# Attention and two gated MLPs on one core: V's global rows loaded into place, V's copies shared with VectorE, and a planner with other prices for the DMA queue

## The chip, the core and the metric

The kernel runs on one core of one Trainium2 chip. The metric is the device time of one execution in microseconds; less is better. TensorE (PE) does the matmuls, VectorE (DVE), ScalarE (ACT) and GpSimd (POOL) the elementwise work, and SyncE (SP) issues every DMA of this kernel, one after the other from one queue.

## The reference, cut to what matters

```python
# batch 4, heads 8, 512 local and 32 global rows per head, head dim 64
out_g = softmax(q_g @ k_all.T / 8) @ v_all          # global rows see everything
s_ll  = where(|i - j| <= 32, q_l @ k_l.T / 8, -1e9) # local rows: a band ...
s_l   = concat([q_l @ k_g.T / 8, s_ll])             # ... and the global keys
out_l = softmax(s_l) @ concat([v_g, v_l])
x = concat([out_g, out_l]) as (2176, 512)           # 4 x 544 tokens
x = x / rms(x) * rms_g
y = (silu(x @ w_gate) * (x @ w_val)) @ w_out        # 512 -> 1536 -> 512
z = (sigmoid(y @ w2_gate) * (y @ w2_val)) @ w2_out  # 512 -> 1536 -> 512
```

The weights arrive as 64-bit floats and are taken apart as two 32-bit words each.

## The kernel before

The local rows are 16 tiles T of 128 rows, four to a batch. Each tile's steps are tasks with names. `lk`, `lq` and `lv` load K, Q and V; `k`, `q` transpose them on TensorE, `kc`, `qc` copy them out of PSUM. `a1` makes the scores of four blocks of 32 rows, each against its band and the 32 global keys, beginning with eight matmuls that write the mask. `mx`, `ex` are row minimum (the scores carry a minus sign) and exponential, `a2` the transpose of the probabilities, `pc` its copy, `a3` the product with V, `nm` the division by the sum. Then follow the RMS norm (`sq`, `ms`, `sc`), the split in two fp16 halves in a staging tile `xs` (`xh` the upper half, `xm` the lower), and `xl`, a transposing DMA from `xs` into the resident operands `xhi`. The global rows of each batch take a path of their own (`sg`, `g1`, `g1x`, `g2`, `g3`, `gx`); `g3` reads V's global rows from a tile `vg`.

For `a3`, V must lie in an order of its own. `vw` is two buffers, even tiles in one and odd tiles in the other; each holds four blocks of keys for the four blocks of rows. A tile of V lies in `vt` (six buffers). Task `("vw", T, n)` copies piece n into `vw`: n = 0 and 1 are 64x1040 elements, n = 2 to 5 are 32x520. Pieces 6 to 9, the global rows, are needed for the first two tiles of a batch alone, since the buffers keep them. Each piece waits until `a3` of tile T-2 has read the buffer. In the kernel before, the four quarters of `vg` are loaded by `load_vg` with four DMAs a batch, and pieces 6 to 9 are copied from there; for T > 1 the planner chooses GpSimd or a DMA for each piece, for T = 0 and 1 GpSimd or VectorE.

The order on all engines is made by a planner in the kernel while it is built. Class `Booked` books each instruction on a clock `now` of its engine with a price; for SP it also books when the data land (`land`). `choose` takes, of the tasks whose inputs are there, the one that can start first within a margin, by priority. Where TensorE would wait longer than `fill`, it puts idle matmuls (`b<-ident` 128x256) in front. Priorities and some prices stand in a table `PR`. `gemm` is a stream of matmuls of the first MLP (`xhi` by `wgv`, then `hhi` and `hlo` by `wo`) that the planner weaves into the attention once `xl` of three tiles has been done. After the attention (`attend`) the rest is written in order, and between matmuls `give` hands out jobs for the other engines: taking weights apart (`c_ops`, `s_ops`) and combinations for a fast product (`jobs`). Nearly every instruction has the line of the recording helper, L145 here and L149 after.

```python
def vw_eng(T, n):
    return "ps" if T > 1 else "pd"
...
        xs_t[T] = ap.tile([128, 2, DM], F16, tag="xs", name="xs", bufs=1)
...
        task(("xh", T), "ad", lambda e: st_xh(T, e), P("xh"), ("sc", T), ref("xl", T - 1), c=(520, 341))
```

Of the kernel before, what the change touches and what calls it, by code (L numbers as in the profile page):

```python
# [10 lines left out]
F32 = mybir.dt.float32  # L11
F16 = mybir.dt.float16
# [9 lines left out]
def tile_attention_moe_moe(  # L22
# [64 lines left out]

    class Booked:
# [4 lines left out]
        def __getattr__(self, name):  # L93
            f = getattr(self.eng, name)

            def g(*args, **kw):
# [3 lines left out]
                ins = [x for x in aps if x is not out]  # L100
                n = max(int(np.prod(x.shape[1:])) for x in aps) if "axis" in kw else int(np.prod(out.shape[1:]))
# [11 lines left out]
                elif key == "s":  # L113
# [9 lines left out]
                    now["s"] = t + (1250 if kw.get("transpose") else 620 if ns[0] < 100000 else 560 + 0.11 * min(max(now["dma"] - t, 0), 6000))  # L123
# [54 lines left out]
    nc = Engines(tc.nc)  # L178
# [955 lines left out]
    def st_g3(b, e):  # L1134
        pt = pt_t.pop(("g", b, e))
        vg = vg_t[b]
        p = bank(("gn", b, e))
        for r in range(5):
            for pr in range(NPR):
                h = 2 * pr + e  # L1140
                if r < 4:
                    l, v = pt[:, r, 32 * pr:32 * pr + 32], vt_t[4 * b + r][:, h * DV:h * DV + D]
                else:
                    l, v = pt[0:SG, r, 32 * pr:32 * pr + 32], vg[0:SG, h * DV:h * DV + D]
                nc.tensor.matmul(p[32 * pr:32 * pr + 32, 0:D], l, v, start=(r == 0), stop=(r == 4))
        p_t["g", b, e] = p
# [45 lines left out]
    def warm(n):  # L1192
        p = bank()
        for i in range(n):
# [3 lines left out]
    PR = dict(lkg=-7.25, kgt=7.41, lqg=-1.98, qgt=3.21, gB=1.07, lk=-4.25, lq=-1.55, lv=-0.02, lg=-0.66,  # L1198
              q=3.87, qc=-16.93, k=0.24, k0=-8.51, nk=-2.48, kc=3.82, kc0=-0.72, a1=8.55, vw=0.09, e=2.04,
              mx=-5.17, ex=2.53, a2=-3.33, pc=-0.11, a3=-0.84, nm=-4.07, sq=15.55, ms=-7.09, sc=-0.86,  # L1200
              a4=-18.55, xh=5.81, xl=-8.54, sg=8.94, g=5.82, lv0=-0.76, lk1=-6.39, G=1000, post=-7.94,
              raw=-3.21, w0=0.24, w1=0.35, w2=12.08, w3=16.91, w4=17.64, w5=-6.83, w6=7.76, w7=26.25,
              w8=11.55, Le=146, Ld=62, La=106, Lp=5314538, Ls=1690, backlog=4477, fill=1035, guard=1, kcd=0,
              land=1190, vs0=24309, vs1=341, vs2=1815, xt=0.37)
# [17 lines left out]
    def ref(name, *a):  # L1222
        return (name, *a) if a[0] >= 0 else None
# [8 lines left out]
    def tile_tasks(T):  # L1232
# [6 lines left out]
        if t == 0:  # L1239
            task(("lg", b), "s", lambda e: load_vg(b), P(PR["lg"]),  # L1240
                 *([("vw", T - 8 + i, n) for i in range(2) for n in range(6, 10)] + [("g3", b - 2, 1)] if b >= 2 else []), after=ref("lg", b - 1))
# [10 lines left out]
        for n in range(len(vw_refs(T))):  # L1252
            v = vw_pieces(T)[n][1]
            task(("vw", T, n), vw_eng(T, n), lambda e, n=n: st_vw(T, n, e), P(PR["vw"]),
                 ref("a3", T - 2, 0), ref("a3", T - 2, 1), ("lg", b) if v is None else ("lv", v),
                 c=(1150 if n < 2 else 606, (616 if n < 2 else 345) if T < 2 else PR["vs0" if n < 2 else "vs1" if n < 6 else "vs2"]))
# [17 lines left out]
        task(("xh", T), "ad", lambda e: st_xh(T, e), P("xh"), ("sc", T), ref("xl", T - 1), c=(520, 341))  # L1274
# [20 lines left out]

    def build_tasks():
        for n, a, dst in (("kg", k_g, kgT), ("qg", q_g, qgT)):
# [12 lines left out]
        task(("xh", NT), "ad", lambda e: st_xh(NT, e), NT, ("sc", NT), ref("xl", NT - 1), c=(520, 341))  # L1310
# [231 lines left out]

    def run_op(key, op):
        e, f = (op.eng, op.f) if isinstance(op, Op) else (op[0] and op[0].lower(), op[1])
        f()
        if e:
            ready[key] = now[e] + 130

    def give():
        while True:  # L1550
            w_give()
            c = []
            for a in (0, 2, 1):
                if part_jobs[a]:
                    c.append((0.0, f"h{a}", part_jobs[a], 0))
            for key, ops in (("c", c_ops), ("s", s_ops)):
                if ops:
                    c.append((due_w(ops), key, ops, 0))
            for k in range(2):
                i = [i for i, x in enumerate(jobs) if x[0][1] == k]  # L1560
                if i:
                    key = jobs[i[0]][0]
                    if k == 0 or not any(x[0] == (key[0], 0) for x in jobs):
                        c.append((due_j(key), key, jobs, i[0]))
            for _, key, js, i in sorted(c, key=lambda x: x[0]):
                op = js[i][1][0] if js is jobs else js[0]
                if fits(key, op):
                    if js is jobs:
                        js[i][1].pop(0)
                        if not js[i][1]:  # L1570
                            js.pop(i)
                    else:
                        js.pop(0)
                    run_op(key, op)
                    break
            else:
                return
# [4 lines left out]
    with tc.manual_schedule():  # L1582
# [17 lines left out]
        w_go[0] = True  # L1600
        for wi, (g, ch, Ts) in list(enumerate(work))[at[0]:]:
# [68 lines left out]
```

## Time and profile before

| | |
|---|---|
| median of 3 runs | 894.03 us |
| lowest, highest | 889.8, 896.12 us |
| the profiled execution, its own time | 896.37 us |
| its span from first to last instruction | 894.5 us |
| mean granted TensorE clock | 0.994 |

The span is the profiled execution seen from inside; its own time holds 1.87 us more, ahead of and behind it. The three timed runs and the profiled one are single executions of the same program. A granted clock of 1 is 2.4 GHz, and the lower level is 1.2 GHz.

### The profile page before, as it was taken

How to read it: one execution, taken by the hardware profiler on the slowest of the kernel's cores; microseconds unless marked ns; L12 is line 12 of the kernel's file. 1: busy time of each engine (PE TensorE's matmuls, PEld its weight loads, DVE VectorE, ACT ScalarE, POOL GpSimd, SP SyncE). 2: the span in 40 equal slices, each digit the busy share in tenths (PEclk: the TensorE clock that was granted, in tenths of full speed). 3: DMA queues.
4: the chain of work that ended last, by engine and by line, in shares of the span. 5: the costliest groups of instructions: out<-in, count | busy, mean ns of one | idle time of the engine just before them, and what ended most of it. 6: DMA issues, size and time to landing. Idle time of an engine off the chain costs nothing.

```text
span 894.5 us, 18832 instructions
## 1 busy us (share of the span) xinstructions
PE 866.8 (97%) x7733; PEld 543.3 (61%) x7733; DVE 610.6 (68%) x1050; ACT 452.2 (51%) x986; POOL 266.7 (30%) x300
## 2 busy tenths in 40 slices
PE   8889798899999999999999999999999999999998
PEld 6667565666666666666666666556556565556553
DVE  4867767697788888788737877748764468645252
ACT  4886586565334445555527444546545264344230
POOL 2754445342211211121214446442202122212010
PEclk9999999999999999999999999999999999999999
DMA  9977879461000114131300121110331003000102
GB/s 211 170 153 145 172 151 185 117 139 63 1 25 23 50 46 124 54 107 48 95 1 1 56 88 48 48 48 28 114 106 37 1 24 95 1 1 13 59 33 98
DMA packets 108998, 66.56 MB, mean 74 GB/s; under 512 B 76912, under 2 KB 101488, under 8 KB 108912
## 3 DMA queue, kind: packets, MB, share of 16 engines
q1 hardware_dynamic: 108912, 65.36, 29.2%
q8 instruction: 61, 1.00, 0.5%
q14 instruction: 25, 0.20, 0.1%
HBM read 52.17 MB, written 4.46 MB: 63 GB/s over the span
## 4 chain that ended last, share of the span: by engine, by line
PE 80%; DMA 9%; DVE 4%; ACT 2%; SPq 1%; issue 1%; POOL 1%; DVEq 0%; ACTq 0%; POOLq 0%
PE p L145 66%; PE b L145 14%; DMA vt<-in_v_l_dram 3%; DMA xhi<-xs 2%; DMA q<-in_q_l_dram 1%; DMA vw<-vt 1%; SPq L145 1%; DVE wf L145 1%; DVE xs L145 1%; DMA k<-in_k_l_dram 1%; ACT s L145 1%; DMA vg<-in_v_g_dram 1%; DVE ya L145 0%; ACT pt L145 0%; DVE wc L145 0%
## 5 line engine op out<-in xcount | busy, mean ns | idle before, releaser
L145 PEld LDWEIGHTS <-wc 128*128 128x128 f16 x2556 | 250.1, 98 | 144.8 <-issue 1.4
L145 PE MATMUL p<-tt,wc 128*128 128x384 f16 (+1 forms) x1296 | 208.6, 317 | 0.6 <-ACT gv L145 0.4
L145 PE MATMUL p<-xhi,wc 128*128 128x384 f16 (+1 forms) x1260 | 205.2, 317 | 0.0
L145 POOL TENSOR_TENSOR h<-gv,h 128x384 f16<-128x384 f32 (+1 forms) x66 | 84.4, 1279 | 286.1 <-ACT h L145 274.1
L145 PE MATMUL p<-wo,h 128*128 128x512 f16 x612 | 133.4, 379 | 0.0
L145 ACT ACTIVATE gv<-p 128x384 f32<-128x384 f32 (+1 forms) x174 | 80.4, 469 | 76.0 <-PE p L145 69.6
L145 DVE SCALAR_TENSOR_TENSOR wf<-raw,wf 128x512 int32<-128x512 int32 x144 | 113.2, 794 | 2.2
L145 PEld LDWEIGHTS <-wo 128*128 128x128 f16 x864 | 84.3, 98 | 47.7 <-issue 0.2
L145 PEld LDWEIGHTS <-h 128*128 128x128 f16 x612 | 59.9, 98 | 71.1
L145 DVE SCALAR_TENSOR_TENSOR ya<-p,ya 128x384 f32<-128x384 f32 (+2 forms) x106 | 61.0, 581 | 54.7 <-PE p L145 53.9
L145 PE MATMUL b<-xhi,wgv 128*128 128x384 f16 (+1 forms) x576 | 93.3, 320 | 2.0 <-DMA xhi<-xs 2.0
L145 ACT ACTIVATE h<-gv 128x384 f16<-128x384 f32 (+3 forms) x93 | 54.7, 592 | 73.5 <-DVE gv L145 71.2
L145 DVE SCALAR_TENSOR_TENSOR gv<-gv 128x384 f32<-128x384 f32 (+3 forms) x81 | 66.7, 823 | 36.2 <-ACT gv L145 35.3
L145 PE MATMUL p<-h,wo 128*128 128x384 f16 (+1 forms) x576 | 90.0, 317 | 0.0
L145 DVE TENSOR_TENSOR gv<-p,gv 128x384 f32<-128x384 f32 (+1 forms) x108 | 55.4, 530 | 46.8 <-ACT gv L145 46.6
L145 PEld LDWEIGHTS <-wgv 128*128 128x128 f16 x576 | 56.2, 99 | 34.6 <-issue 1.8
L145 ACT ACTIVATE sa<-p 128x384 f32<-128x384 f32 (+1 forms) x54 | 24.7, 466 | 79.2 <-PE p L145 79.0
L145 ACT ACTIVATE wf<-raw 128x512 f32<-128x512 f32 x72 | 47.2, 671 | 27.9 <-DVE wc L145 13.5
L145 POOL COPY vw<-vt 64x1040 f32<-64x1040 f32 (+1 forms) x37 | 39.5, 1069 | 50.2 <-DMA vt<-in_v_l_dram 38.7
L145 POOL TENSOR_TENSOR sm<-wf 128x256 f32<-128x256 f32 x18 | 15.4, 858 | 119.9 <-DVE wc L145 87.3
L145 POOL TENSOR_TENSOR hlo<-t,hhi 128x384 f16<-128x384 f32 (+1 forms) x24 | 26.6, 1109 | 69.3 <-ACT hhi L145 69.1
L145 PE MATMUL b<-hhi,wo 128*128 128x384 f16 (+1 forms) x192 | 46.9, 317 | 0.0
(117 smaller groups left out, 1007.1 us busy)
## 6 DMA issues: line engine op xcount, KB each, us to landing
raw<-in_moe_w_gate_dram SPq DMA_DIRECT2D x24, 512.0 KB, 4.1
raw<-in_moe_w_val_dram SPq DMA_DIRECT2D x24, 512.0 KB, 3.7
raw<-in_moe_w_out_dram SPq DMA_DIRECT2D x24, 512.0 KB, 3.7
k<-in_k_l_dram SPq DMA_DIRECT2D x16, 256.0 KB, 3.9
q<-in_q_l_dram SPq DMA_DIRECT2D x16, 256.0 KB, 4.9
vt<-in_v_l_dram SPq DMA_DIRECT2D x16, 256.0 KB, 5.3
out_dram<-ya SPq DMA_DIRECT2D x16, 256.0 KB, 2.0
vw<-vt SPq DMA_DIRECT2D x54, 65.0 KB, 2.8
```

The source lines that it names most:

```text
L145: return f(*args, **kw)
```

## The change

Pieces 6 to 9 of `vw` are no longer copied from `vg`: each is a DMA from V's global rows in HBM straight into the buffer, always on SP. The column of ones beside V is written once into both buffers by a new task `ones`. `vg` is loaded once a batch instead of four times. The other pieces of tiles above 1 may now go to VectorE too (`"psd"`). `xs` gets a second buffer, and `xh` waits for `xl` of tile T-2 rather than T-1. The planner prices a DMA issue at 700 ns (620 before) or 620 ns and a share of the backlog (560), a transposing one at 1600 ns (1250), and a landing at 2243 ns after the data (1190). All numbers of `PR` are others, so the whole order of the attention moves. Behind the attention, `fill_in` is called before each instruction of VectorE or ScalarE that would wait, and puts a job into that wait if it fits. Of the new functions, `handout` and `take` are `give`'s old code cut out.

```diff
@@ class Booked
+                if key in "da" and between[0]:
+                    between[0](key, max([wrote.get(tag_of(x), 0.0) for x in ins] + [free0.get(out.tensor.name, 0.0)]))
...
-                    now["s"] = t + (1250 if kw.get("transpose") else 620 if ns[0] < 100000 else 560 + 0.11 * min(max(now["dma"] - t, 0), 6000))
+                    now["s"] = t + (1600 if kw.get("transpose") else 700 if ns[0] < 100000 else 620 + 0.11 * min(max(now["dma"] - t, 0), 6000))
@@ load_vg
-        vg_t[b] = ap.tile([128, H * DV], F32, tag="vg", name="vg", bufs=2)
-        nc.gpsimd.memset(vg_t[b].rearrange("p (h d) -> p h d", h=H)[:, :, D:DV], 1.0)
-        for i in range(4):
-            nc.sync.dma_start(out=vg_t[b][32 * i:32 * i + SG].rearrange("p (h d) -> p h d", h=H)[:, :, 0:D],
-                              in_=v_g[b].rearrange("h p d -> p h d"))
+        vg_t[b] = ap.tile([128, H, D], F32, tag="vg", name="vg", bufs=1)
+        nc.sync.dma_start(out=vg_t[b][0:SG], in_=v_g[b].rearrange("h p d -> p h d"))
@@ vw_eng, st_vw
-        return "ps" if T > 1 else "pd"
+        return "s" if n >= 6 else "psd" if T > 1 else "pd"
...
-        i = (vg_t[T // TPB] if v is None else vt_t[v])[r]
+        if v is None:
+            nc.sync.dma_start(out=o.rearrange("p (h d) -> p h d", h=H)[:, :, 0:D], in_=v_g[T // TPB].rearrange("h p d -> p h d"))
+            return
+        i = vt_t[v][r]
@@ st_xh
-        xs_t[T] = ap.tile([128, 2, DM], F16, tag="xs", name="xs", bufs=1)
+        xs_t[T] = ap.tile([128, 2, DM], F16, tag="xs", name="xs", bufs=2)
@@ PR (one line of nine)
-              w8=11.55, Le=146, Ld=62, La=106, Lp=5314538, Ls=1690, backlog=4477, fill=1035, guard=1, kcd=0,
+              Lp=570650794, Ls=1558, backlog=5956, fill=2110, guard=1, kcd=0, land=2243, vs0=28709, vs1=0,
@@ tile_tasks
-        task(("xh", T), "ad", lambda e: st_xh(T, e), P("xh"), ("sc", T), ref("xl", T - 1), c=(520, 341))
+        task(("xh", T), "ad", lambda e: st_xh(T, e), P("xh"), ("sc", T), ref("xl", T - 2), c=(520, 341))
@@ new
+    def st_ones():
+        for w in vw:
+            nc.gpsimd.memset(w.rearrange("p i (h d) -> p (i h) d", d=DV)[:, :, D:DV], 1.0)
+    def fill_in(e, t):
+        while t > now[e] + 200:
+            for _, key, js, i in handout():
+                ...
+                s = max([now[e], 0 if free else ready.get(key, 0)] + [wrote.get(tag_of(x), 0.0) for x in (ins() if ins else ())])
+                if s + took.get(f.__code__, 900) <= t + 250:
+                    take(key, js, i)
+                    break
+            else:
+                return
@@ behind the attention
         w_go[0] = True
+        between[0] = fill_in
```

Counted over the whole program, the instructions that change in number are these. TensorE: 59 fewer idle matmuls (29 instead of 88). VectorE: copies of 64x1040 into `vw` 16 instead of 2, of 32x520 3 instead of 6, and copies of `ptg` 8 instead of 5. GpSimd: 16 instead of 30 and 18 instead of 26. SP: loads of `vg` 4 instead of 16, loads of V's global rows into `vw` 32 instead of 0, copies of `vt` into `vw` 43 instead of 54, of `vg` into `vw` 0 instead of 10; 245 DMAs instead of 246.

SyncE's queue at the program's start, before (`x` holds the global K or Q rows, `raw` a half of a weight block, numbers tell buffers apart):

```order
L145 DMA k_144<-in_k_l_dram 128x8x64
L145 DMA k_146<-in_k_l_dram 128x8x64
L145 DMA raw_148<-in_moe_w_gate_dram 128x4x256
L145 DMA raw_155<-in_moe_w_gate_dram 128x4x256
L145 DMA raw_158<-in_moe_w_val_dram 128x4x256
L145 DMA k_185<-in_k_l_dram 128x8x64
L145 DMA x_191<-in_q_g_dram 32x8x64 x4
L145 DMA raw_200<-in_moe_w_val_dram 128x4x256
L145 DMA q_209<-in_q_l_dram 128x8x64
```

The same place after:

```order
L149 DMA k_146<-in_k_l_dram 128x8x64
L149 DMA k_148<-in_k_l_dram 128x8x64
L149 DMA x_150<-in_q_g_dram 32x8x64 x4
L149 DMA vt_163<-in_v_l_dram 128x8x64
L149 DMA q_172<-in_q_l_dram 128x8x64
L149 DMA k_180<-in_k_l_dram 128x8x64
L149 DMA raw_187<-in_moe_w_gate_dram 128x4x256
L149 DMA raw_198<-in_moe_w_gate_dram 128x4x256
L149 DMA raw_201<-in_moe_w_val_dram 128x4x256
L149 DMA vg_206<-in_v_g_dram 32x8x64
L149 DMA q_226<-in_q_l_dram 128x8x64
```

The load of the global Q rows, of V's first tile and of Q's first tile have moved ahead of the weights.

SyncE's queue around the first three transposing DMAs, before (here the second and the third stand, those of tiles 1 and 2):

```order
L145 DMA k_980<-in_k_l_dram 128x8x64
L145 DMA vt_995<-in_v_l_dram 128x8x64
L145 DMA q_1021<-in_q_l_dram 128x8x64
L145 DMA k_1034<-in_k_l_dram 128x8x64
L145 DMA vt_1083<-in_v_l_dram 128x8x64
L145 DMA_TRANSPOSE xhi0_73<-xs_1053 128x8x128
L145 DMA vw0_85<-vt_995 32x520 x3
L145 DMA vw0_85<-vg_729 32x520
L145 DMA vw0_85<-vt_1083 32x520
L145 DMA vw1_86<-vt_995 32x520
L145 DMA vw1_86<-vt_1083 32x520 x2
L145 DMA_TRANSPOSE xhi0_73<-xs_1258 128x8x128
```

After (all three stand here):

```order
L149 DMA vt_827<-in_v_l_dram 128x8x64
L149 DMA q_851<-in_q_l_dram 128x8x64
L149 DMA_TRANSPOSE xhi0_73<-xs_840 128x8x128
L149 DMA_TRANSPOSE xhi0_73<-xs_842 128x8x128
L149 DMA vg_965<-in_v_g_dram 32x8x64
L149 DMA vw0_85<-vt_655 32x520 x2
L149 DMA vw0_85<-vt_827 32x520
L149 DMA vw0_85<-in_v_g_dram 32x8x64 x2
L149 DMA_TRANSPOSE xhi0_73<-xs_1087 128x8x128
L149 DMA vw0_85<-in_v_g_dram 32x8x64 x2
```

The first two transposes now stand side by side, behind the loads of tile 6's Q, and the third follows six DMAs later; some of V's global rows are loaded ahead of it.

VectorE where the first `xs` tiles are made, before (`gmx`, `ptg` belong to the global rows):

```order
L145 COPY pt_1025<-b_975 128x512
L145 COPY ptg_1005<-b_987 32x128
L145 SCALAR_TENSOR_TENSOR x_747<-x_747,ms_993,gB_80 128x512
L145 CAST xs_1053<-x_747 128x512
L145 TENSOR_REDUCE gmx_1055<-b_1007 128x1
L145 TENSOR_REDUCE gmx_1055<-b_1008 128x1
L145 TENSOR_TENSOR gmx_1055<-gmx_1055 128x1
```

After:

```order
L149 SCALAR_TENSOR_TENSOR x_532<-x_532,ms_609,gB_80 128x512
L149 SCALAR_TENSOR_TENSOR x_701<-x_701,ms_771,gB_80 128x512
L149 CAST xs_840<-x_532 128x512
L149 CAST xs_842<-x_701 128x512
L149 TENSOR_TENSOR xs_840<-x_532,xs_840 128x512
L149 TENSOR_TENSOR xs_842<-x_701,xs_842 128x512
```

Two `xs` tiles are now made one inside the other, where before one stands alone.

## Rows read from the trace of the kernel before

**Rows 1.** The profile's page, part 1: busy time of each engine, share, instructions.

```profile
PE 866.8 (97%) x7733; PEld 543.3 (61%) x7733; DVE 610.6 (68%) x1050; ACT 452.2 (51%) x986; POOL 266.7 (30%) x300
```

**Rows 2.** Busy time in six stretches: length, engines, granted clock, DMA share, GB/s.

```profile
0.00:20.00 20.00, 17.73 (x131) 13.52 (x131) 8.97 (x15) 9.17 (x20) 4.28 (x26) 1.00 0.97 217
20.00:50.00 30.00, 26.71 (x808) 20.90 (x812) 25.98 (x59) 25.13 (x87) 20.50 (x33) 1.00 0.90 173
50.00:100.00 50.00, 43.91 (x1052) 32.42 (x1050) 33.32 (x78) 34.59 (x106) 27.05 (x42) 0.97 0.76 152
100.00:165.00 65.00, 54.97 (x1136) 38.57 (x1135) 44.90 (x94) 42.57 (x118) 33.75 (x46) 0.95 0.85 172
...
200.00:880.00 680.00, 679.44 (x4208) 411.43 (x4206) 464.89 (x751) 318.53 (x610) 168.07 (x139) 1.00 0.16 49
```

**Rows 3.** What TensorE waited for, 0 to 200 us: total us, times, longest.

```profile
PE b L145 <- DMA q<-in_q_l_dram: 6.3, 5, 2.6
PE b L145 <- DMA vw<-vt: 4.4, 5, 3.0
PE b L145 <- DMA xhi<-xs: 2.0, 2, 1.1
PE b L145 <- DVE wo L145: 1.8, 1, 1.8
PE b L145 <- DMA k<-in_k_l_dram: 1.8, 2, 1.5
```

**Rows 4.** TensorE in order of time: start, duration, instructions, wait ahead.

```profile
7.68 6.28 PE L145 MATMUL b<-ident 128*128 128x256 bf16 x56
...
19.65 0.30 PE L145 MATMUL b<-mask,ident 64*32 64x256 bf16 x8
...
31.62 1.41 PE L145 MATMUL b<-vw,pt 128*32 128x65 f32 x58
...
175.93 0.62 PE L145 MATMUL b<-vw,pt 128*32 128x65 f32 x20
```

**Rows 5.** SyncE's queue in order of time: start, duration, DMAs issued.

```profile
0.72 1.89 SPq L145 DMA_DIRECT2D x<-in_k_g_dram  x4
2.65 1.08 SPq L145 DMA_DIRECT2D k<-in_k_l_dram  x2
3.77 1.45 SPq L145 DMA_DIRECT2D raw<-in_moe_w_gate_dram  x2
...
7.85 3.69 SPq L145 DMA_DIRECT2D x<-in_q_g_dram  x4
```

**Rows 6.** Stretches of 5 us in which the granted clock was low.

```profile
55.00:60.00 5.00, 5.00 (x145) 4.32 (x147) 2.80 (x7) 3.74 (x13) 3.07 (x5) 0.74 0.51 117
...
140.00:145.00 5.00, 5.00 (x88) 3.05 (x87) 0.37 (x4) 2.10 (x7) 3.54 (x6) 0.70 1.00 155
...
160.00:165.00 5.00, 5.00 (x105) 3.86 (x94) 3.67 (x8) 1.40 (x3) 3.64 (x3) 0.66 0.91 217
```

**Rows 7.** Instructions that write vw: count, ns minimum/median/maximum, first and last.

```profile
L145 SPq DMA_DIRECT2D vw<-vt x54: 507/541/2257, 33.4 to 163.0; - x54
L145 POOL COPY vw<-vt x37: 606/1047/1981, 21.5 to 162.3; 64x1040 f32<-64x1040 f32 x30, 32x520 f32<-32x520 f32 x7
...
L145 DVE COPY vw<-vt x5: 684/751/1549, 21.7 to 31.4; 32x520 f32<-32x520 f32 x3, 64x1040 f32<-64x1040 f32 x2
```

**Rows 8.** VectorE's waits for the transposing DMA, 0 to 200 us.

```profile
DVE xs L145 <- DMA xhi<-xs: 8.2, 4, 4.6
```

**Rows 9.** SyncE's waits for TensorE, 0 to 200 us.

```profile
SPq L145 <- PE b L145: 25.8, 23, 2.8
```

**Rows 10.** The view of DMA issues: count, KB each, median us to landing.

```profile
q<-in_q_l_dram SPq DMA_DIRECT2D x16, 256.0 KB, 4.9
...
vw<-vt SPq DMA_DIRECT2D x54, 65.0 KB, 2.8
...
vg<-in_v_g_dram SPq DMA_DIRECT2D x16, 64.0 KB, 3.4
```

More of the change, by code (lines that the diff above doesn't have):

```diff
@@ L86, in fetched @@
         return came[min(i, len(came) - 1)] if i >= 0 else 0.0
+    between = [None]
     class Booked:
@@ L1143, in st_g3 @@
                 else:
-                    l, v = pt[0:SG, r, 32 * pr:32 * pr + 32], vg[0:SG, h * DV:h * DV + D]
+                    l, v = pt[0:SG, r, 32 * pr:32 * pr + 32], vg[0:SG, h]
                 nc.tensor.matmul(p[32 * pr:32 * pr + 32, 0:D], l, v, start=(r == 0), stop=(r == 4))
@@ L1240, in tile_tasks @@
             task(("lg", b), "s", lambda e: load_vg(b), P(PR["lg"]),
-                 *([("vw", T - 8 + i, n) for i in range(2) for n in range(6, 10)] + [("g3", b - 2, 1)] if b >= 2 else []), after=ref("lg", b - 1))
+                 *([("g3", b - 1, 0), ("g3", b - 1, 1)] if b else []), after=ref("lg", b - 1))
         task(("q", T), "e", lambda e: tr4(("q", T), q_t.pop(T).rearrange("p h d -> p (h d)"), ("qc", T)), P(PR["q"]), ("lq", T), ref("a1", T - 2) if PR["guard"] else None, banks=1)
@@ L1253, in tile_tasks @@
             v = vw_pieces(T)[n][1]
-            task(("vw", T, n), vw_eng(T, n), lambda e, n=n: st_vw(T, n, e), P(PR["vw"]),
-                 ref("a3", T - 2, 0), ref("a3", T - 2, 1), ("lg", b) if v is None else ("lv", v),
-                 c=(1150 if n < 2 else 606, (616 if n < 2 else 345) if T < 2 else PR["vs0" if n < 2 else "vs1" if n < 6 else "vs2"]))
+            vd = PR["vd"]
+            task(("vw", T, n), vw_eng(T, n), lambda e, n=n: st_vw(T, n, e), P(PR["vw" if n < 6 else "vz"]),
+                 ref("a3", T - 2, 0), ref("a3", T - 2, 1), ("ones",) if v is None else ("lv", v),
+                 c=(0,) if n >= 6 else (1150 if n < 2 else 606, 616 + vd if n < 2 else 345 + vd) if T < 2 else
+                 (1150 if n < 2 else 606, PR["vs0" if n < 2 else "vs1"], 616 + vd if n < 2 else 345 + vd))
         for e in range(2):
@@ L1294, in batch_tasks @@
         task(("gxc", b), "ad", lambda e: st_gxc(b, e), P(8), ("gx", b), c=(525, 607))
+    def st_ones():
+        for w in vw:
+            nc.gpsimd.memset(w.rearrange("p i (h d) -> p (i h) d", d=DV)[:, :, D:DV], 1.0)
     def build_tasks():
+        task(("ones",), "p", lambda e: st_ones(), PR["k0"])
         for n, a, dst in (("kg", k_g, kgT), ("qg", q_g, qgT)):
@@ L1541, in fits, with handout, take @@
         return free or ready.get(key, 0) <= t
+    took = {}
     def run_op(key, op):
         e, f = (op.eng, op.f) if isinstance(op, Op) else (op[0] and op[0].lower(), op[1])
-        f()
+        t = e and now[e]
+        b, between[0] = between[0], None
+        f()
+        between[0] = b
+        if e:
+            took[f.__code__] = now[e] - t
         if e:
             ready[key] = now[e] + 130
+    def handout():
+        c = []
+        for a in (0, 2, 1):
+            if part_jobs[a]:
+                c.append((0.0, f"h{a}", part_jobs[a], 0))
+        for key, ops in (("c", c_ops), ("s", s_ops)):
+            if ops:
+                c.append((due_w(ops), key, ops, 0))
+        for k in range(2):
+            i = [i for i, x in enumerate(jobs) if x[0][1] == k]
+            if i:
+                key = jobs[i[0]][0]
+                if k == 0 or not any(x[0] == (key[0], 0) for x in jobs):
+                    c.append((due_j(key), key, jobs, i[0]))
+        return sorted(c, key=lambda x: x[0])
+    def take(key, js, i):
+        op = js[i][1].pop(0) if js is jobs else js.pop(0)
+        if js is jobs and not js[i][1]:
+            js.pop(i)
+        run_op(key, op)
+    def fill_in(e, t):
+        while t > now[e] + 200:
+            for _, key, js, i in handout():
+                op = js[i][1][0] if js is jobs else js[0]
+                eng, ins, free, f = (op.eng, op.ins, op.free, op.f) if isinstance(op, Op) else (op[0] and op[0].lower(), None, op[0] == "A", op[1])
+                if eng != e or key[0] == "h" or isinstance(op, Op) and op.ok and not op.ok():
+                    continue
+                s = max([now[e], 0 if free else ready.get(key, 0)] + [wrote.get(tag_of(x), 0.0) for x in (ins() if ins else ())])
[4 more added lines that the diff above has]
+                return
     def give():
@@ L1551, in give @@
             w_give()
[L1552 to L1574, printed above, removed]
+            for _, key, js, i in handout():
+                if fits(key, js[i][1][0] if js is jobs else js[0]):
+                    take(key, js, i)
                     break
```

14 lines of the change are left out of this document (7 added, 7 removed).

## The prediction

> **What bounds the kernel now.** I began with the busy times: TensorE is busy for 866.8 us of the span, 97%, and no other engine passes 68% [rows 1]. Time can be won only where TensorE does not work, or does idle work. The stretches say where that is [rows 2]: from 200 to 880 us it is busy for 679.44 of 680 us, and the DMA engines are at 0.16. In the first 165 us it is busy for 143.25 us (17.73 + 26.71 + 43.91 + 54.97) and idle for 21.75, with the DMA engines at 0.76 to 0.97. The weaving of attention and first MLP is the place; the waits name what ended the idle time there: loads of Q, 6.3 us, copies into vw, 4.4, transposes into xhi, 2.0, loads of K, 1.8, and a weight half that VectorE made late, 1.8 [rows 3]. Most are a DMA that came later than the planner had thought, while other matmuls would have been free to run.
>
> Busy is not all useful. Of the idle matmuls 56 stand in one row from 7.68 to 13.96 us, 112 ns each [rows 4]; they cover a wait. And in three places the granted clock is 0.74, 0.70 and 0.66, partly on the lower level [rows 6], each just behind a wait for Q or vw: 0.26 + 0.30 + 0.34 of 5 us are 4.5 us of clock.
>
> One simplification: the last product with V runs at 175.93 us [rows 4], and behind it the program's matmuls are the same in number but for six more after the change, a microsecond. The end moves with what TensorE loses ahead of that point.
>
> **The start.** Before, the first scores begin at 19.65 us [rows 4], since K's third load, the global Q rows and the first Q queue behind weights: halves of 512 KB go out from 3.77 us on, and the global Q rows' four issues take 3.69 us behind them, against 1.89 for K's four in an empty queue [rows 5]. After, the order puts global Q rows, V and Q ahead of the weights. K's two loads end at 3.73 us; global Q takes 1.89 to 3.69, V and Q 0.54 each (1.08 for two [rows 5]); so Q is issued by 6.7 to 8.5 us and lands 4.9 later [rows 10], 11.6 to 13.4. From the first Q's transposes to the first scores I allow 1.5 us, an estimate of one transpose and one copy. So the scores begin at 13 to 15 us, 5 to 7 earlier.
>
> The first product with V, at 31.62 [rows 4], needs V's second tile and the four global pieces, now loads. Up to the last of them the order has 4928 KB, 5.05 MB. At 217 GB/s 4.34 MB are moved by 20 us, the other 0.71 take 4.1 us at 173 GB/s [rows 2]: 24 to 25 us, some 6.6 earlier. This doesn't last. The order shows about 9.5 MB up to Q of tile 6 in both kernels, which by the same rates is 50 us either way, and TensorE reaches it behind nearly the same blocks. What it gained by starting early it waits for there, unless the queue, idle for a tenth of 20 to 50 us (3 us), closes up. I take 3 us of gain, ends 0 and 6.6. The 59 idle matmuls removed are worth nothing of their own: they stood in waits. The clock was granted in full through 0 to 50 us [rows 2]; with 29 left it could fall once, as in rows 6, for some 1.5 us; that is inside the ends.
>
> **V's copies.** The 14 further 64x1040 copies on VectorE cost 0.68 us each where it is alone, 1.55 at most [rows 7]: 10 to 22 us of an engine busy for 104 of the 145 us from 20 to 165 (25.98 + 33.32 + 44.90 [rows 2]). At 10 it is at 79%; the free fifth hides them, and they run in place of GpSimd copies of 1.05 us. Against that, work that TensorE waits for queues behind them, so +1 us, ends 0 and +4 (four copies of 1 us on the path).
>
> **V's global rows.** 32 loads replace 12 loads of vg and 10 copies of it, and 11 copies of vt leave the queue: one DMA less, about the same bytes. A vg load lands in 3.4 us, a vw copy in 2.8 [rows 10]: 0.6 more where one ends a wait; the load no longer waits for a vg. But more of the queue must now wait in it for a product that reads the buffer: 43 + 32 = 75 DMAs instead of 64. SP's waits for TensorE were 25.8 us in 23 [rows 9], 1.1 each, and behind a waiting issue stand the loads of the next Q, K and V. 11 more by 25.8/64 are 4.4 us of SP; a third of that reaches TensorE in my guess: +1.5, ends 0 and +12 (all eleven at 1.1).
>
> The Trainium skill, "DMA: Bandwidth & Descriptors", section "Why small descriptors are slow (HBM only)", speaks against this edit: runs of 256 bytes from HBM carry 27% overhead, transfers inside SBUF don't. A row of V is such a run; the 20 further loads are 1.31 MB, 7.6 us at 173 GB/s, so by the rule an estimated 1.6 us more, and the forecast would be 887.6. The rows agree in direction only: 3.4 against 2.8 us to landing [rows 10].
>
> **The second xs.** VectorE stood for 8.2 us in four waits until a transpose had read xs [rows 8], everything behind it in the queue too, the late weight half and the following transposes among it. The second buffer ends that; late next is the norm ahead of it. TensorE's part is at most 2.0 + 1.8 us [rows 3]; I take -2, ends 0 and -3.8.
>
> **The planner's prices.** A landing is now booked a microsecond later and issues 60 to 350 ns dearer. In the trace issues take 0.51 to 2.26 us [rows 7] and Q 4.9 to land, so this is nearer to the rows. TensorE's order is fixed when built; a better guess puts other matmuls ahead of a Q that isn't there. At stake is 6.3 + 4.4 + 1.8 = 12.5 us [rows 3]. Most of the queue is itself full (0.76 to 0.90 [rows 2]) and reordering doesn't make it faster, so I take -4, a third; ends 0 and -12.5. With fewer long waits a third of the clock's 4.5 us comes back, -1.5.
>
> **Jobs in waits.** Behind 200 us TensorE lacks 0.56 us [rows 2]; earlier jobs on VectorE and ScalarE have nothing to give. Cost zero, bounded by the rival below.
>
> **Sum.** -3 + 1 + 1.5 - 2 - 4 - 1.5 = -8 us. Against the profiled execution's 896.37 us that is 888.4; this one lay 2.3 us above the median of 894.03, so what a median would show is 886.0.
>
> **Rivals.** (1) *DMA in lockstep.* The queue of SP and its engines set the pace to 165 us (0.97, 0.90, 0.76, 0.85 [rows 2]); bytes and DMAs are equal, so the early start is waited for at tile 6 and new waits replace old ones; only about 1 us of xs remains: 893. For: the equal bytes. Against: a tenth to a quarter of DMA time is free. (2) *The waits go.* Prices now fit: start -5, xs -3.8, two thirds of the loads' waits -8, clock -3, costs +3, together -16.8: 877. For: TensorE has matmuls of the first MLP to run in any wait from about 65 us. (3) *Head of the queue.* A global piece for a batch's first two tiles stands in SP's queue until a product has read the buffer, and loads wait behind. Price 1.1 us each; if all eleven further waits reach TensorE, +12, with only the start's -3 against it: 903. It decides from about 8 us of added waiting, where the rest of the gain is gone. (4) *Jobs in the way.* A job put in front of a PSUM evacuation delays the next product; at 0.6 us in each of the 30 products of a block and a chunk behind 200 us, +18, less the 8: 904. Against: eight banks, and 0.56 us lost there now.
>
> **How the numbers follow.** About 1% is what a measurement of this kernel tells from no change: below 885.1 or above 903.0. The forecast, 886.0 with its own range 881 to 891, has 0.47, of it 0.20 below 885.1. Rival 1 has 0.23, all within 1%. Rival 2 has 0.18, all faster. Rivals 3 and 4 together have 0.12, 0.09 of it slower. So faster 0.38, same 0.53, slower 0.09. The range that leaves out a fifth reaches to rival 2's middle and the weaker half of rivals 3 and 4: 877 to 899.
>
> **What would show it.** The first scores near 13 to 15 us and the first product with V near 25; no wait of VectorE's xs for the transposing DMA; TensorE's waits for Q, K and vw below 10 us together; fewer stretches at the lower clock; still under 1 us lost from 200 to 880. I am wrong if scores begin early but the idle time up to 165 us stays near 22 us (rival 1), if SP's waits for TensorE grow past 35 us (rival 3), or if waits appear behind 200 us (rival 4).

## The result, and the profile after

The changed kernel takes 881.47 us (median of four runs, 880.91 to 881.8) where the kernel before took 893.38 beside it (four runs, 889.8 to 896.12). The ratio is 0.9868 with a 95% interval of 0.9832 to 0.9905: 11.9 us, or 1.3%, faster. The forecast of 886.0 was 4.5 us too slow; the time lies within its range and at the edge of its own 881 to 891. The profiled execution took 881.62 us against 896.37, a span of 879.8 us against 894.5.

First the page's part 1 of the kernel after:

```profile
PE 855.5 (97%) x7674; PEld 535.0 (61%) x7674; DVE 621.2 (71%) x1069; ACT 448.7 (51%) x980; POOL 243.6 (28%) x274
```

TensorE's busy time fell by 11.3 us against [rows 1], though it does the same useful work; its idle time inside the span fell only from 27.7 us to 24.3. Most of the gain is therefore busy time that went: 59 idle matmuls at 112 ns are 6.6 us, and the clock gives about 1.2 more (below); the other 3.5 are not assigned here. An idle matmul stands where there would have been a wait, so that part is only another name for a wait; where the work itself came earlier the stretches say, in the columns of [rows 2]:

```profile
0.00:20.00 20.00, 14.70 (x147) 9.93 (x148) 8.85 (x15) 10.56 (x27) 7.63 (x32) 1.00 1.01 214
20.00:50.00 30.00, 24.32 (x758) 19.20 (x761) 26.06 (x59) 21.64 (x70) 13.30 (x22) 0.95 0.96 190
50.00:100.00 50.00, 45.38 (x1010) 32.58 (x995) 40.61 (x90) 35.32 (x106) 22.82 (x37) 1.00 0.80 165
100.00:165.00 65.00, 62.21 (x1426) 45.56 (x1419) 55.69 (x125) 49.93 (x146) 23.43 (x39) 1.00 0.82 163
165.00:200.00 35.00, 35.00 (x241) 23.40 (x239) 32.84 (x53) 20.93 (x42) 9.87 (x10) 1.00 0.44 120
```

TensorE is busy for less time than before up to 50 us and for more from there to 200: 62.21 of 65 us from 100 to 165, against 54.97. The idle time up to 165 us is 18.4 us (21.75 before). Note the DMA rate from 20 to 50 us: 190 GB/s, where before it was 173.

What ended TensorE's idle time from 0 to 200 us, after, as in [rows 3]:

```profile
PE b L149 <- DMA k<-in_k_l_dram: 4.2, 4, 1.8
PE b L149 <- issue: 3.9, 8, 1.0
PE b L149 <- DMA q<-in_q_l_dram: 2.3, 3, 1.4
...
PE b L149 <- POOL vt L149: 1.4, 1, 1.4
```

Loads of Q fell from 6.3 us to 2.3, no DMA into `vw` is waited for any more (4.4 before), and the late weight half is gone; loads of K rose from 1.8 to 4.2. The last line is a product with V that starts right behind a GpSimd copy into `vw` and the memset of `vt` after it. The three kinds together are 6.5 us instead of 12.5, below the 10 that I had named as the sign; the experiments show below how little that sign tells. TensorE in order of time, after, as in [rows 4], with the first scores proper (`kTr` by `qT`), and below them two lines of the kernel before that [rows 4] leaves out:

```profile
11.70 0.30 PE L149 MATMUL b<-mask,ident 64*32 64x256 bf16 x8
12.54 1.15 PE L149 MATMUL b<-kTr,qT 64*32 64x128 f32 x64 [0.55 <-ACT qT L149]
...
26.34 1.13 PE L149 MATMUL b<-vw,pt 128*32 128x65 f32 x64
...
51.23 0.66 PE L149 MATMUL b<-ident,q 128*128 128x128 f32 x4
...
158.25 0.67 PE L149 MATMUL b<-vw,pt 128*32 128x65 f32 x32
...
469.69 5.09 PE L149 MATMUL p<-tt,wc 128*128 128x320 f16 x24 [2.05 <-ACT gv L149]
```

```profile
20.19 1.15 PE L145 MATMUL b<-kTr,qT 64*32 64x128 f32 x64 [0.23 <-DVE qT L145]
...
53.40 0.63 PE L145 MATMUL b<-ident,q 128*128 128x128 f32 x4 [1.49 <-DMA q<-in_q_l_dram]
```

The mask's matmuls, which read no Q, come 8.0 us earlier than before, the first scores proper 7.7, tile 6's Q 2.2, the first product with V 5.3, the last one 17.7. From there to the end it is 2.9 us longer than before (720.9 against 717.9). Six matmuls more are in it, a new wait of 2.05 us at 469.69, the last line of the first fence, for ScalarE's `gv`, and the low clock behind that wait. SyncE's start, after, shows why the scores come early (compare [rows 5]):

```profile
0.73 1.88 SPq L149 DMA_DIRECT2D x<-in_k_g_dram  x4
2.65 1.08 SPq L149 DMA_DIRECT2D k<-in_k_l_dram  x2
3.77 2.42 SPq L149 DMA_DIRECT2D x<-in_q_g_dram  x4
6.23 0.45 SPq L149 DMA_DIRECT2D vt<-in_v_l_dram  x1
6.73 0.58 SPq L149 DMA_DIRECT2D q<-in_q_l_dram  x1
```

Q goes out at 6.73 us, as worked out (6.7 to 8.5). SyncE's waits for TensorE, and the instructions that write `vw`, after, as in [rows 9] and [rows 7]:

```profile
SPq L149 <- PE b L149: 14.3, 23, 2.1
```

```profile
L149 SPq DMA_DIRECT2D vw<-vt x43: 513/541/1722, 29.6 to 148.7; - x43
L149 POOL COPY vw<-vt x34: 606/952/1576, 10.0 to 146.7; 32x520 f32<-32x520 f32 x18, 64x1040 f32<-64x1040 f32 x16
L149 SPq DMA_DIRECT2D vw<-in_v_g_dram x32: 396/492/2921, 17.0 to 137.9; - x32
L149 DVE COPY vw<-vt x19: 423/699/1546, 10.0 to 146.9; 64x1040 f32<-64x1040 f32 x16, 32x520 f32<-32x520 f32 x3
```

The queue holds 75 DMAs into `vw` instead of 54 and 10, and yet waits less for TensorE: 14.3 us instead of 25.8. The three stretches of 5 us at a low clock [rows 6] are gone; two others stand there, one behind the start and one behind the new wait for `gv`:

```profile
20.00:25.00 5.00, 3.82 (x84) 2.68 (x87) 4.30 (x7) 1.50 (x5) 2.35 (x4) 0.68 0.98 230
...
470.00:475.00 5.00, 5.00 (x26) 3.09 (x25) 3.31 (x6) 1.42 (x4) 0.96 (x1) 0.66 0.01 3
```

They cost 0.32 + 0.34 of 5 us, 3.3, where before it was 4.5 in three places: 1.2 us come back. The second one lies behind 200 us; from 200 to 880 us the kernel before has none below 1.00.

### The profile page after: what moved, and what is told of

Same layout as the page of the kernel before. It is cut to its first block, busy times and chain, and to the rows that moved or that the text cites. A ratio compares the mean times of both kernels' runs of the same rounds, so it can differ in the third digit from the quotient of the medians.

```text
span 879.8 us, 18699 instructions
## 1 busy us (share of the span) xinstructions
PE 855.5 (97%) x7674; PEld 535.0 (61%) x7674; DVE 621.2 (71%) x1069; ACT 448.7 (51%) x980; POOL 243.6 (28%) x274
## 4 chain that ended last, share of the span: by engine, by line
PE 89%; DMA 3%; DVE 3%; ACT 2%; issue 1%; SPq 1%; POOL 1%; DVEq 0%; POOLq 0%
PE p L149 67%; PE b L149 22%; DMA k<-in_k_l_dram 2%; SPq L149 1%; DMA q<-in_q_l_dram 1%; DVE gv L149 1%; DVE x L149 0%; DVE wc L149 0%; DVE xhi L149 0%; ACT h L149 0%; ACT gv L149 0%; ACT wc L149 0%; POOL ms L149 0%; DVE gmx L149 0%; DVE mx L149 0%
## 5 line engine op out<-in xcount | busy, mean ns | idle before, releaser
L149 POOL TENSOR_TENSOR h<-gv,h 128x384 f16<-128x384 f32 (+1 forms) x66 | 86.3, 1308 | 300.1 <-ACT h L149 287.1
L149 DVE SCALAR_TENSOR_TENSOR wf<-raw,wf 128x512 int32<-128x512 int32 x144 | 109.0, 766 | 2.1
L149 DVE SCALAR_TENSOR_TENSOR gv<-gv 128x384 f32<-128x384 f32 (+3 forms) x81 | 70.5, 870 | 41.6 <-ACT gv L149 40.8
L149 POOL TENSOR_TENSOR hlo<-t,hhi 128x384 f16<-128x384 f32 (+1 forms) x24 | 24.1, 1004 | 77.8 <-ACT hhi L149 77.8
L149 ACT ACTIVATE gv<-gv 128x384 f32<-128x384 f32 (+1 forms) x81 | 40.0, 494 | 3.2 <-DVE gv L149 2.8
```

The source lines that it names most:

```text
L149: return f(*args, **kw)
```

## The experiments

Two kinds of kernel are told apart here. In one the planner makes a new order, since a price, a number of its table or a task has changed. In the other, called *frozen*, the plan is booked as in the kernel it starts from, and only the instruction named is another one, so that all else keeps its place in its engine's order. Every ratio is against the kernel before, run on the same chip beside it (medians 893.16 to 894.29). A difference between two experiments is given as one of their medians. My theory was the prediction's: the gain is the planner's better picture of SyncE's queue, with small parts from the start, `xs` and the clock. The rivals now were that the gain is the start and V's way into `vw`, or that it is only a table that fits better.

**The planner's prices, in both directions.** In the kernel before, the issue prices and the landing of the kernel after, nothing else; in the kernel after, the old ones.

```diff
 e6_before_newprices (e5_after_oldprices is the reverse, in the kernel after)
-  now["s"] = t + (1250 if transpose else 620 if ns[0] < 100000 else 560 + ...)
+  now["s"] = t + (1600 if transpose else 700 if ns[0] < 100000 else 620 + ...)
-  land=1190
+  land=2243
```

> The kernel before planned with the new prices for issues and landings, its table of priorities otherwise its own. My theory: 4 us less than before (0 to 7), TensorE's waits for Q, K and vw below 10 us. Rival: priorities were fitted to the old prices, and new prices alone give another plan of the same worth or a worse one: between 2 us less and 8 us more than before.

> The changed kernel planned with the old prices: 620, 560 and 1250 ns for an issue and a landing of 1190 ns; the table of priorities is the new one. My theory: the prices are worth 4 us (0 to 12.5) and what is left of the gain once the start (6.8 us by the run with weights first) and the jobs (1.7 us lost) are taken out is 6.8 us: so 4 to 7 us more than the changed kernel, with TensorE's waits for Q, K and vw up. Rival: the priorities and the start carry the gain, a plan with other prices is only another plan: within 3 us of the changed kernel, either way.

The kernel before with new prices takes 887.46 us (five runs), ratio 0.9932 [0.9909, 0.9956], 6.8 us faster. The kernel after with old ones takes 901.06, ratio 1.0076 [1.0058, 1.0094], 19.6 us slower than after itself. The reverse shows less than its number: the table of after was made with the new prices, so old prices also break the fit between table and plan, which by the controls below costs 5 to 7 us by itself. For the kernel before with new prices, the waits of TensorE from 0 to 200 us are:

```profile
PE b L145 <- issue: 5.7, 10, 1.0
...
PE b L145 <- DMA k<-in_k_l_dram: 0.6, 2, 0.4
PE b L145 <- DMA vw<-vt: 0.5, 1, 0.5
```

and its stretches from 50 us on:

```profile
50.00:100.00 50.00, 46.83 (x1135) 34.49 (x1120) 39.14 (x90) 39.25 (x127) 30.21 (x47) 1.00 0.94 169
100.00:165.00 65.00, 60.81 (x1342) 43.76 (x1340) 50.17 (x113) 46.01 (x128) 35.61 (x53) 1.00 0.78 158
```

The 12.5 us of waits for Q, `vw` and K [rows 3] have become 1.1; TensorE is busy for 8.8 us more in these two stretches (107.64 against 98.88; 0.6 of it are four idle matmuls) and the clock there is whole. All of this with the old start (the mask's matmuls at 20.21 us), one `xs` and the old way of V. "Issue", time that waits for nothing the profile shows, takes the first place.

**How far such a result is the price's own.** A new plan differs from the old one in hundreds of places, and the table of priorities was there with another plan. Three kernels ask how much any change of plan moves.

```diff
 e11_before_jit, e10_after_nofill_jit: every priority of the table moved by a tenth of a tile
+  for i, x in enumerate(sorted(priorities)):
+      PR[x] += (-0.1, 0.1)[(i * 7 // 3) % 2]
 e12_before_land: in the kernel before, the landing alone
-  land=1190
+  land=2243
```

> The kernel before with every priority moved by 0.1 of a tile up or down, prices the old ones: the control for the run in which only the prices were new (6.8 us less than before). My theory: the old prices keep the waits for Q, K and vw above 10 us, and the time is that of before within 3 us or worse. Rival: any other plan of the kernel before can lie 7 us lower, and the prices are not what did it.

> The changed kernel without jobs in waits, planned with every priority of the table moved by 0.1 of a tile up or down; prices the same. It measures what another plan of the same kind costs. If the order is robust: within 3 us of 879.8. If the table is fitted to a single plan: 4 us or more slower, with new waits of TensorE between 20 and 165 us.

> The kernel before planned with the later landing alone (2243 ns instead of 1190), issue prices the old ones. My theory: the landing is the part of the prices that keeps TensorE from standing before a load that is not there: 4 to 7 us less than before, the waits for Q, K and vw under 6 us. Rival: the issue prices, which let the queue run later in the plan, carry it: within 2 us of before.

The kernel before with moved priorities: 898.32 us (eleven runs), ratio 1.0050 [1.0027, 1.0073], 5.2 slower. The kernel after without its jobs in waits (the kernel e4 below), with moved priorities: 886.73, 6.9 slower than e4. The landing alone in the kernel before: 898.92, ratio 1.0059 [1.0037, 1.0080], 5.8 slower. So each of the two tables fits its own plan, and one disturbance of each cost 5 and 7 us. The new prices gained 6.8 us with a table that was not made for them; in the kernel before the two other disturbances both lost. That speaks against a lucky plan but doesn't exclude one: two controls are few, and the gain is no larger than what they lost.

The waits by name do not tell these plans apart. Those for Q, `vw` and K are 6.1 us in e11 and 6.5 in e12, half of the 12.5 before (for e11 I had expected more than 10), and both kernels are slower than before; in e5 they are 7.3, against 6.5 in after, and it takes 19.6 us more. Other losses took their place:

```profile
PE b L145 <- ACT s L145: 6.7, 3, 2.9
...
178.82 7.26 PE L145 MATMUL b<-ident 128*128 128x256 bf16 x65
```

The first line is e11's largest wait, the second stands in e12. What goes with the time is TensorE's idle time and its idle matmuls together, over the whole span: 38.1 us before, 31.1 in e6, 27.8 in after, but 40.9 in e11, 41.0 in e5 and 44.6 in e12. In e12 the last product with V begins 9.5 us earlier than before (166.39 against 175.93), and the loss lies behind it, where 65 idle matmuls stand ahead of matmuls that read `xhi`. So the landing alone does not gain, but that it does nothing for the attention is not shown either; whether the dearer issues gain alone or only with it stays open.

**The code without the table.** The kernel after with the old table and landing, but its new code and issue prices.

```diff
 e9_after_oldtable
-  PR = dict(lkg=-6.67, kgt=8.24, ..., fill=2110, land=2243, vs0=28709, ...)
+  PR = dict(lkg=-7.25, kgt=7.41, ..., fill=1035, land=1190, vs0=24309, ..., vd=297.21, vz=0.54)
```

> The changed kernel's code (global V loaded in place, V copies on three engines, two xs tiles, new issue prices, jobs in waits) planned with the old table of priorities and the old landing of 1190 ns; the weights stand ahead of the global Q rows again. If the gain comes from the start and the plan: about the time of before or worse, 890 to 897. If the code's edits carry it: 884 or less.

904.61 us, ratio 1.0124 [1.0091, 1.0156]: 11 us slower than the kernel before. Since the new issue prices stand beside the old landing here, a pair that no other run has, and the old table was made for the old code, this does not price the edits; it says only that they gain nothing with these numbers.

**The start.** The kernel after, frozen, with three weight halves issued ahead of the global Q rows, near to where the kernel before has them.

```diff
 e3_after_weights_first, at the load of the global Q rows
+  for i in range(3):                       # two halves of w_gate, one of w_val
+      tc.nc.sync.dma_start(out=early[i], in_=weight half i)
   load_g(n, a)
   ... (the three later issues are left out)
```

> The changed kernel with its order kept on all engines, except that the first three weight halves are issued ahead of the global Q rows, as before, instead of behind the third load of K. My term for the start: 3 us more than the changed kernel (0 to 6.6), with the first scores at 18 to 20 us instead of 11.7. The lockstep rival: the DMA queue sets the pace, the first scores come late, but by 50 us the lag is gone and the time is that of the changed kernel within 1 us. If the start is worth all that it shows, 5 to 7 us more.

888.23 us (six runs), ratio 0.9941 [0.9918, 0.9964]: 6.8 us slower than after. Its TensorE in order of time:

```profile
18.64 0.41 PE L150 MATMUL b<-mask,ident 64*32 64x256 bf16 x8
...
60.36 0.66 PE L150 MATMUL b<-ident,q 128*128 128x128 f32 x4
...
164.87 0.67 PE L150 MATMUL b<-vw,pt 128*32 128x65 f32 x32
```

Against after it is 6.9 us late at the first scores, 9.1 at tile 6's Q and 6.6 at the last product with V. The lag does not heal. From 20 to 50 us its DMA engines run at 0.67 and 144 GB/s, so they are not what holds it there. A part may be the clock, 0.74 from 0 to 20 us and 0.89 from 20 to 50 (1.00 and 0.95 in after).

**V's copies on GpSimd again.** After, frozen; the 15 copies of tiles above 1 that VectorE makes go to GpSimd.

```diff
 e8_after_vcopy_pool, in st_vw
-  nc.vector.tensor_copy(out=o, in_=i)
+  nc.gpsimd.tensor_copy(out=o, in_=i)    # where T > 1
```

> The changed kernel with its order kept, but V's copies on VectorE for tiles above 1 (15 of them) stand on GpSimd at the same places. My step: VectorE hides them at a cost of 1 us on the path: so GpSimd, idle for 70%, hides them as well, within 2 us of the changed kernel, a little faster if VectorE was in the way. Rival: the copies on VectorE are what lets V arrive in time (0.7 us instead of 1.05 and no queue behind a copy that waits for a load): 3 to 7 us slower, with new waits of TensorE for vw.

885.88 us (five runs), ratio 0.9903 [0.9881, 0.9925]: 4.4 us slower than after. The largest wait of TensorE is new, and the timeline of this kernel shows how it comes about, TensorE first, then VectorE, then GpSimd (L932 is the line of the moved copies):

```profile
48.33 1.08 PE L150 MATMUL b<-vt,ptg 128*32 128x64 f32 x32 [4.00 <-DVE den L150]
...
43.25 0.75 DVE L150 SCALAR_TENSOR_TENSOR x<-x,ms,gB 128x512 f32<-128x512 f32 x1 [1.92 <-POOL ms L150]
43.92 2.47 DVE L150 CAST xs<-x 128x512 f16<-128x512 f32 x2
...
47.51 0.68 DVE L150 COPY ptg<-b 128x512 f32<-128x512 f32 x1
...
39.74 2.51 POOL L932 COPY vw<-vt 64x1040 f32<-64x1040 f32 x2
42.34 0.22 POOL L150 TENSOR_SCALAR ms<-ms 128x1 f32<-128x1 f32 x1
42.64 0.57 POOL L150 TENSOR_TENSOR ms<-ms,mhalf 128x1 f32<-128x1 f32 x1
...
43.81 2.30 POOL L150 COPY vw<-vt 64x1040 f32<-64x1040 f32 x2 [0.53 <-PE b L150]
```

Two moved copies hold GpSimd to 42.3 us; behind them stands the small work on `ms`, for which VectorE's norm waits 1.92 us; then VectorE makes `xs`, and only behind that come the copy of `ptg`, which the late product reads, and the `den` that the bracket names. One queue holds up the next, three engines long. Behind that wait the granted clock falls, to 0.58 from 50 to 55 us where after has 1.00, so more is lost than the wait itself:

```profile
50.00:55.00 5.00, 5.00 (x129) 4.46 (x125) 2.57 (x7) 3.24 (x8) 1.40 (x3) 0.58 0.85 99
```

And the two casts take 2.47 us beside GpSimd's copies; in the kernel after, in the same place, with GpSimd idle, they take 0.76:

```profile
41.86 0.76 DVE L149 CAST xs<-x 128x512 f16<-128x512 f32 x2
```

**V's global rows from SBUF.** After, frozen; the 32 loads of V's global rows into `vw` read `vg` in SBUF, with a DMA of the same size from the same place of the queue.

```diff
 e7_after_vg_sbuf, in st_vw
-  nc.sync.dma_start(out=o, in_=v_g[T // TPB])        # HBM
+  nc.sync.dma_start(out=o, in_=vg_t[T // TPB][0:SG]) # SBUF
```

> The changed kernel with its order kept, but V's global rows go into vw by the same 32 queue entries from the one copy in SBUF (vg) rather than from HBM. I put both within 0.6 us of landing of each other: within 1 us of the changed kernel, up to 2 us slower since the first pieces must wait for vg to land. By the Trainium skill (DMA: Bandwidth & Descriptors, Why small descriptors are slow) transfers inside SBUF lack the overhead of 256-byte runs from HBM: an estimate of 2.6 us less DMA time for 32 loads, so up to 2.6 us faster.

885.51 us (five runs, 883.15 to 888.26), ratio 0.9894 [0.9872, 0.9917]: 4.0 us slower than after. In the views of DMA issues and of the instructions that write `vw`, the copy from SBUF here, then the load of the kernel after:

```profile
vw<-vg SPq DMA_DIRECT2D x32, 64.0 KB, 3.7
L923 SPq DMA_DIRECT2D vw<-vg x32: 590/612/1777, 17.6 to 144.3; - x32
...
vw<-in_v_g_dram SPq DMA_DIRECT2D x32, 64.0 KB, 3.2
```

The copy lands in 3.7 us at the median, the load in 3.2; and SyncE takes 612 ns at the median to issue the copy, 492 for the load, 3.8 us over all 32. What the 4 us of the kernel are made of is not settled: the clock is lower in three stretches (0.91, 0.94 and 0.95), and SyncE waits 2.1 us for `vg` itself, which the load does not.

**The second `xs`.** The kernel before, frozen; `xs` of the odd tiles 1 to 9 lies in an unused piece of another buffer, so that the tiles follow each other without waiting for the transpose.

```diff
 e1_before_xs2
-  xs of T: the one buffer xs
+  xs of T in (1, 3, 5, 7, 9): yacc[1][:, 2560:3072], as two halves of f16
```

> The kernel before with its order of instructions kept, but tiles 1, 3, 5, 7 and 9 put their two halves into a second place (an unused stretch of yacc), so that a copy into xs no longer waits for the transpose of the tile before. My term for the second xs: 2 us less than before (0 to 3.8), and VectorE's 8.2 us of waits for the transposing DMA nearly gone up to tile 10. Rival: those waits are off the path, since the order of TensorE and of the queue is fixed by the plan; then the time is that of before within 1 us although the waits go.

893.25 us (twelve runs) beside 893.66, ratio 0.9999 [0.9978, 1.0021]: nothing. VectorE's wait for the transposing DMA falls only from 8.2 us in four [rows 8] to this,

```profile
DVE xs L146 <- DMA xhi<-xs: 4.8, 1, 4.8
```

and TensorE's waits for `xhi` are 2.7 us (2.0 before). The wait that is left ends at 145.67 us, in one of the last tiles, where this kernel still has the one buffer; before, the same one is 4.6 of the 8.2. So the run shows that the three shorter waits, 3.6 us, are worth nothing, and leaves the longest untried. In the order of the kernel after the second buffer can't be taken away, since two `xs` tiles are made one inside the other there; its worth in that order was not tried.

**The idle matmuls.** The kernel before, frozen, all 88 left out (none of their results is used).

> The kernel before with its order kept, but none of its 88 idle matmuls is issued. My step says that they stand in waits and are worth nothing of their own: within 1 us of before, the idle time at the start 9 us longer instead; up to 1.5 us slower if the clock falls once at the start. Rival: they hold up what stands behind them (the profile after is busy 6.5 us less by the 59 that went): then up to 6 us less than before.

893.73 us (twelve runs), ratio 1.0010 [0.9991, 1.0030]: nothing, although the clock of the first stretches fell, where [rows 2] have 1.00:

```profile
0.00:20.00 20.00, 9.98 (x49) 6.00 (x49) 9.10 (x15) 9.32 (x20) 4.28 (x26) 0.77 1.03 221
20.00:50.00 30.00, 25.95 (x769) 21.56 (x763) 24.69 (x52) 24.00 (x82) 20.48 (x32) 0.92 0.82 154
```

The waits for K in that kernel are 9.1 us, 5.8 the longest: where TensorE has to wait for loads, a slow clock ahead of them can be paid for out of the wait. The run does not tell this from a second reading, in which the idle matmuls that went gave back what the clock cost.

**The jobs in waits.** The kernel after without them.

```diff
 e4_after_nofill
-  between[0] = fill_in
```

> The changed kernel without jobs put into waits behind the attention; the attention's order is the same. My term: zero, within 1 us of the changed kernel. The rival of jobs in the way: the one wait of 2.0 us behind 200 us, for a ScalarE copy of gv, which the kernel before does not have, goes with them: 2 us less than the changed kernel. If the jobs help, more than 1 us slower.

879.8 us (four runs, 879.6 to 880.2), ratio 0.9846 [0.9819, 0.9874]. It is the fastest kernel of all, 1.7 us below after. All its four runs are below all of after's four, but the two were run on different occasions and their intervals of the ratio overlap. Its timeline has, in place of the wait of 2.05 us at 469.69, two short ones:

```profile
320.99 4.06 PE L149 MATMUL p<-tt,wc 128*128 128x384 f16 x24 [0.78 <-ACT gv L149]
...
469.34 3.42 PE L149 MATMUL p<-tt,wc 128*128 128x320 f16 x24 [0.20 <-ACT gv L149]
```

That is 1.1 us less of waiting, and from 470 to 475 us its clock is 1.00 instead of 0.66, another 1.7; from 20 to 50 us its clock is lower than after's (0.89 against 0.95), which takes some of it back. Which job stood ahead of `gv` was not looked into further.

## Why the prediction was right, term by term

The case forecast is the one that came: attention and the woven first MLP get tighter up to 165 us, and behind 200 us little changes. The sum was -8 us and measured are -11.9; the sizes of the terms were worse than their sum, so that the time came out so near is partly luck.

- *The prices, -4.* This is the most mis-sized term as far as e6 shows. A third of the 12.5 us of waits was to go, since reordering doesn't make a full queue faster. In the kernel before the new prices gain 6.8 us, and the waits fall to 1.1. The DMA rate from 50 to 165 us was no ceiling: it was 152 and 172 GB/s in the two stretches before, and TensorE did 8.8 us more work there at 169 and 158, about the same bytes moved earlier. But the step from fewer waits for loads to less time is not general: in e11 and e12 half of these waits went and the time rose. What the prices give in the plan of after is not shown.
- *V's copies on VectorE, +1, and V's global rows, +1.5.* The first has the wrong sign in the order of the kernel after: taking it back costs 4.4 us. I had costed what queues behind VectorE and not what is freed behind GpSimd, where `ms` stood behind copies; nor that the two engines slow each other. For the second I had priced 11 further waits at the head of the queue; the waits fell to 14.3 us instead, with more DMAs in the same queue. What the edit as a whole is worth was not tried: e7 keeps all 32 DMAs in the queue and changes only where they read, which costs 4.0 us. Since both experiments are frozen, they also undo some of the fit between order and prices, which by the controls can be worth as much as the 4 us; so the sign is shown for this order, the size of the edit by itself isn't.
- *The rule on small descriptors* (the Trainium skill, "DMA: Bandwidth & Descriptors", "Why small descriptors are slow (HBM only)") would have had the 32 copies from SBUF faster by an estimated 2.6 us (1.6 for the 20 further loads of the prediction). The Trainium skill reckons 3 cycles of 11 there, so its 27% is a share of the whole time, and the two estimates should have been 3.3 and 2.1 us. Measured, the same 32 pieces from SBUF land later (3.7 against 3.2 us) and the kernel is 4.0 us slower; the rule did not decide here.
- *The start, -3.* Up to 26 us the row-by-row account held: Q issued at 6.73 (6.7 to 8.5 worked out), first product with V at 26.34 (24 to 25); the first scores came earlier than the 13 to 15, at 12.54, since Q's transposes began at 11.11 (11.6 to 13.4 worked out); the step from them to the scores took 1.4 us, where I allowed 1.5. The rows at 19.65 and 11.70, which the prediction calls the first scores, are the mask's matmuls, which need no Q and ran while its copy out of PSUM was under way. That the lead would be gone at tile 6 was nearly right by its rows, 2.2 us are left of it (51.23 against 53.40). But it rested on 173 GB/s as the queue's rate, and that is what the kernel before asked for: the kernel after moves 190 there, and e3 144. In its own order the early start is worth 6.8 us (e3); in e6 an order without it gains as well. It is not a term that can be added to the others.
- *The second `xs`, -2.* Three of VectorE's four waits are worth nothing in the order before (e1); the longest, and the second buffer in the new order, were not tried. The sign that I named held: the kernel after has no wait of VectorE's `xs` for the transposing DMA.
- *The clock, -1.5.* It is -1.2 in the profiled executions, two low stretches instead of three.
- *The idle matmuls, 0.* Right in the order before (e2).
- *The jobs in waits, 0.* They cost 1.7 us by the medians of e4 and after, in the way of rival 4, in one place instead of 30. Here a sign of mine failed: not under 1 us but some 2 are lost from 200 us on, in one wait, and the low clock behind it adds 1.7.

With the measured sizes in place of the guessed ones the sum moves by -2.8 (prices), -2.5 (V's edits taken as costing nothing), +0.3 (clock), +2 (`xs`) and +1.7 (jobs), to -9.3. It is no account of the 11.9: the terms overlap (the 6.8 of e6 and the 1.7 of e4 have clock in them), they were measured in two orders, and the same code under the old table is 11 us slower than before, not faster.

Of the rivals, lockstep (893) fell: the idle time up to 165 us, its sign, went from 21.75 us to 18.4, with 6.9 us of idle matmuls gone beside it; from 20 us on it went from 19.4 to 13.1. The head of the queue (903) fell with the 14.3 us. Of the case that the waits go (877) the waits came three quarters of the way, 6.0 us less where it had 8; its 3.8 us for `xs` were nothing in e1. Open are which of the price's two parts gains, whether the prices carry the gain in the plan of after or the table fitted with them does, and what the second `xs` is worth in the new order.

## What to carry to other kernels

Where a planner fixes the order on each engine, the time that it books for issuing and landing a DMA can be worth as much as an edit of the work: here the new prices moved one plan by 6.8 us, and the waits for loads shrank though the queue got no faster. One of the two prices alone lost 5.8, so try them together and singly. Judge such plans by all the idle time and idle matmuls of the engine that bounds the kernel; the waits for one kind of load fell in faster and slower plans alike. A rate that a stretch shows is what the order asked for, not what the DMA engines can give, unless they are at full share there. And take an edit back within the new order before calling it a gain or a cost, with a disturbed plan beside it as a control: here one disturbance of each table cost 5 and 7 us, as much as most edits.

## What the hardware showed beside it

Two of VectorE's casts of a 128x512 tile to f16 took 0.76 us with GpSimd idle and 2.47 beside GpSimd's copies of 64x1040 (rows of e8 and after above); the copies took 1.15 us each in that place, and 1.04 to 1.05 where they were shortest. The issue of one and the same small load on SyncE took 0.40 us at the least and 2.92 at the most (the 32 loads into `vw` above). A wait of TensorE costs more than its length where the clock falls behind it: 2.05 us, and then 0.66 over 470 to 475 us, in the kernel after; 4.00 us, and then 0.58 over 50 to 55, in e8. And with the idle matmuls left out, a granted clock of 0.77 over the first 20 us made no difference to the time that could be measured (e2).
